# A three-part kernel on one core: work recorded as operations and list-scheduled inside the kernel, in place of loops ordered by the compiler's scheduler

## The chip, the core and the metric

The kernel runs on one core of a Trainium2 chip. The core has five engines that run on their own: TensorE (PE in the profile, with its weight loads as PEld), VectorE (DVE), ScalarE (ACT), GpSimd (POOL) and SyncE (SP), which here issues every transfer (DMA). Each engine works through its own queue in order: an instruction that waits holds up all that stands behind it on that engine. The metric is device time of one execution in microseconds (us), lower is better.

## The reference, cut to what matters

```python
scores = q @ k.T / sqrt(64)                  # 2 batches, 8 heads, 576 rows, 64 wide
kth = the 32nd largest score of each row
attn = softmax over the scores >= kth        # the others count as nothing
x = (attn @ v), heads side by side           # 1152 tokens x 512
h = x @ moe_w_in                             # 512 -> 2048
g = h * tanh(softplus(h))
x = g @ moe_w_out                            # 2048 -> 512
out = ((x @ w_a) * (x @ w_b)) @ w_out        # 512 -> 1536 twice, 1536 -> 512
```

Data and results are float32. The weights of both MLPs come to the device as 64-bit words, and the kernel turns them into float32 itself.

## The kernel before, in words

**Tiles.** The 1152 tokens are nine tiles of 128 rows, t = 0 to 8. For every tile attention goes through four pairs of heads, hp = 0 to 3, so there are 36 steps.

**Attention.** `scores` makes the query parts qh and ql and four score products psc for each step (L170), which ACT copies into the tile s2 (L172). `largest` then finds the 32nd largest score with four rounds on DVE: MAX8 (L186) takes the eight largest, MATCH_REPLACE8 (L189) strikes them out. That makes 8 MAX8 and 6 MATCH_REPLACE8 in each step. `weighted_sum` masks and exponentiates (L206 on DVE, L192, L211 and L212 on ACT), transposes on PE (pe, L219), multiplies by v (px, L225 and L228), and after the fourth pair divides by the sums: prs on PE (L240), then x on DVE (L242). In this document x3 and x8 are the results x of the fourth and of the ninth tile.

**Weights.** `convert` reads each of 68 weight blocks (128 x 512, 512 KB as 64-bit words), turns it into float32 and stores it to device memory (ws, 256 KB): two or three ACT instructions (L285, L286, L289), a shift on DVE (L287), then an integer add and a multiply by the sign on POOL (L290, L291). For nine blocks DVE merges the sign instead (L293). `weight` loads a stored block again (raw, 256 KB) each time that a group of tiles needs it. For the tiles that use split operands it makes two parts of it, whl: a high part by a cast (L321 on ACT or L319 on DVE) and the rest by a subtraction (L322 on POOL or DVE). Which engine does it follows counters (`phase`, `sub`).

**MLPs.** SEQ is the list of groups: the gated MLP (kind 1) for tiles 0, 1 and 2, each alone and unsplit, then the bilinear MLP (kind 2) for tiles 0 to 2 together, gated for 3 to 5, bilinear for 3 to 5, gated for 6 to 8, bilinear for 6 to 8. From the first bilinear group on operands are split, three matmuls for one product. The products are ph (L349), the sums acc and po (L363, L371). The gate's multiplication is L410 in the gated MLP and L445 in the bilinear one; `gate_parts` splits the result into gh (ACT, L378) and gl (L379).

**Order.** Three sources of work (attention, conversion, MLP) are generators. A loop at the end of the kernel keeps a clock of DVE, ACT and PE, with rounded costs (PACE, `cost`), and steps the source whose clock is lowest. The compiler's own scheduler then orders the instructions of all engines by priority (`tc.high_priority(PRI[...])`) and by its own model of time; it also moves single matmuls between each other.

Of the kernel before, what the change touches and what calls it, by code (L numbers as in the profile page):

```python
# [9 lines left out]
F32 = mybir.dt.float32  # L10
# [8 lines left out]
P = 128  # L19
U = 512  # L20
TOPK = 32


SEQ = [(1, [0], 0, 0, 1, 0), (1, [1], 0, 0, 4, 0), (1, [2], 0, 0, 0, 0), (2, [0, 1, 2], 1, 4, 0, 0), (1, [3, 4, 5], 1, 4, 0, 0), (2, [3, 4, 5], 1, 4, 1, 0), (1, [6, 7, 8], 1, 4, 4, 2), (2, [6, 7, 8], 1, 4, 0, 1)]

PACE = (2.8, 1.0, 0.8, 1.65, 0.315, 0.0, 16.0)

PRI = (200, 444, 30, 0, 37, 100)

PS = (3, 2, 3)  # L30


KSUB = (0, 0)

SIGN = (4, 3)

ABUF = (5, 3, 2, 1, 2, 3, 1, 2)
BUFS = (3, 9, 9, 6, 1)

WIDE = {2 * P: 2, P: 4}  # L40
NEG = -3.0e38
STEEP = 2.0 ** 100
# [3 lines left out]
def topk_attention_mlps(ctx: ExitStack, tc: tile.TileContext, q, k, v, w, out):  # L46
# [9 lines left out]
    F1, F2 = 16, 12  # L56
# [8 lines left out]
    const = ctx.enter_context(tc.tile_pool(name="const", bufs=1))  # L65
    stg = ctx.enter_context(tc.tile_pool(name="stg", bufs=2))
    att = ctx.enter_context(tc.tile_pool(name="att", bufs=2))
    xp = ctx.enter_context(tc.tile_pool(name="xp", bufs=1))
    wp = ctx.enter_context(tc.tile_pool(name="wp", bufs=1))
    ep = ctx.enter_context(tc.tile_pool(name="ep", bufs=ABUF[5]))  # L70
    dp = ctx.enter_context(tc.tile_pool(name="dp", bufs=1, space=DRAM))
    ps = ctx.enter_context(tc.tile_pool(name="ps", bufs=PS[0], space=PSUM))
    ps_h = ctx.enter_context(tc.tile_pool(name="ps_h", bufs=PS[1], space=PSUM))
    ps_a = ctx.enter_context(tc.tile_pool(name="ps_a", bufs=PS[2], space=PSUM))

    kks = const.tile([P, H + 2, S], F32R, name="kks")
# [3 lines left out]
    nc.vector.memset(half, 0.5)  # L80

    def bank(name, n=512):
        return ps.tile([P, n], F32, name=name, tag="bank", padded_shape=[P, 512])

    nc.scalar.preload_act_table_set("natural_log_exp_and_others")
    vt, v4, KK, QQ, X, XR = {}, {}, {}, {}, {}, {}

    def load_v(b):
        vt[b] = const.tile([P, H, J, D], F32, name=f"v{b}")
        v4[b] = const.tile([P, NP, 2, D], F32, name=f"v4{b}")  # L90
        nc.gpsimd.memset(v4[b], 0.0)
        for h in range(H):
            nc.sync.dma_start(vt[b][:, h], v[b, h, 0:SM, :].rearrange("(p j) d -> p j d", j=J))
        for s in range(2):
            nc.sync.dma_start(
                v4[b][s * R:(s + 1) * R, :, s, :],
                v[b, :, SM:S, :].rearrange("(a s) p d -> s p a d", s=2)[s],
            )

    def prep_k(b, hp):  # L100
        ks = wp.tile([P, 2, J, D], F32, name="ks", bufs=BUFS[4])
        kr = wp.tile([R, 2, D], F32, name="kr", bufs=BUFS[4])
        for s in range(2):
            nc.sync.dma_start(ks[:, s], k[b, 2 * hp + s, 0:SM, :].rearrange("(p j) d -> p j d", j=J))
        nc.sync.dma_start(kr, k[b, 2 * hp:2 * hp + 2, SM:S, :].rearrange("h p d -> p h d"))
        km = wp.tile([P, 2, J, 2, D], F32R, name="km", bufs=BUFS[4])
        kn = wp.tile([R, 2, 2, D], F32R, name="kn", bufs=BUFS[4])
        for z, raw in ((km, ks), (kn, kr)):
            high, low = (z[..., i, :] for i in range(2))
            nc.scalar.copy(high, raw)  # L110
            (nc.gpsimd, nc.vector)[KSUB[b]].tensor_sub(low, raw, high.bitcast(F32))
        for s in range(2):
            kk = kks[:, (b * H + 2 * hp + s) % (H + 2), :]
            pk = bank("pk")
            for j in range(J):
                nc.tensor.transpose(pk[:, j * P:(j + 1) * P], km[:, s, j].rearrange("p z d -> p (z d)").bitcast(F32),
                                    ident)
            pr = bank("pr", R)
            nc.tensor.transpose(pr, kn[:, s].rearrange("p z d -> p (z d)").bitcast(F32), ident[:R, :R])
            for src, o, n in ((pk, s * R, SM), (pr, SM * (1 - s), R)):  # L120
                nc.scalar.copy(kk[:, o:o + n], src)  # L121
            KK[b, 2 * hp + s] = kk

    def load_q(t):
        qr = stg.tile([P, H, 2, D], F32, name="qr", bufs=1)
        for z in range(2):
            if t == J:
                for b in range(B):
                    nc.sync.dma_start(qr[b * R:(b + 1) * R, :, z, :], q[b, :, SM:S, :].rearrange("h p d -> p h d"))
            else:  # L130
                rows = q[t // (J + 1), :, 0:SM, :].rearrange("h (p j) d -> j p h d", j=J)
                nc.sync.dma_start(qr[:, :, z, :], rows[t % (J + 1)])
        QQ[t] = qr

    def prep_q(t, hp):
        pq = bank("pq", 2 * P).rearrange("p (s t) -> p s t", t=P)
        for s in range(2):
            nc.tensor.transpose(pq[:, s, :], QQ[t][:, 2 * hp + s, :, :].rearrange("p z d -> p (z d)"), ident)
        made = []
        for b, o, n in ([(t // (J + 1), 0, P)] if t != J else [(b, b * R, R) for b in range(B)]):  # L140
            qh = att.tile([P, 2, P], F32R, name="qh", bufs=ABUF[4])
            ql = att.tile([P, 2, P], F32R, name="ql", bufs=ABUF[4])
            if n != P:
                z = slice((1 - b) * R, (2 - b) * R)
                nc.gpsimd.memset(qh[:, :, z].bitcast(F32), 0.0)
                nc.gpsimd.memset(ql[:, :, z].bitcast(F32), 0.0)
            dh, dl, src = (z[:, :, o:o + n] for z in (qh, ql, pq))
            nc.scalar.mul(dh, src, SCALE)
            nc.vector.scalar_tensor_tensor(dl, src, SCALE, dh.bitcast(F32), op0=ALU.mult, op1=ALU.subtract)
            made.append((b, qh, ql))  # L150
        return made

    def scores(t, hp):
        with tc.high_priority(PRI[0]):
            return scores_(t, hp)

    def scores_(t, hp):
        if hp == 0:
            load_q(t)
        made = prep_q(t, hp)  # L160
        if t in (0, J):
            prep_k(t // J, hp)
        s2 = att.tile([P, 2, S], F32, name="s2", bufs=ABUF[0])
        for s in range(2):
            h = 2 * hp + s
            parts = [(qq, KK[b, h]) for b, qh, ql in made for qq in (qh, ql)]
            for a in range(2):
                psc = bank("psc", HS)
                for n, (qq, kk) in enumerate(parts):
                    nc.tensor.matmul(psc, qq[:, s, :], kk[:, a * HS:(a + 1) * HS],  # L170
                                     start=(n == 0), stop=(n == len(parts) - 1))
# [407 lines left out]
```

## Time and profile before

| | before |
|---|---|
| median of three runs | 774.36 us (770.68 to 776.7) |
| the profiled execution's own time | 773.75 us |
| its span, first to last instruction | 771.9 us |
| busy: PE / DVE / ACT / POOL | 679.2 / 581.2 / 542.2 / 469.3 us |
| granted clock of PE, mean | 0.956 |
| moved by DMA | 131.37 MB |

How to read the rows. A group of instructions stands in one line: its line in the kernel, engine, operation, output and inputs by the program's names, count, time busy and mean time of one. What is to the right of an arrow to the left (<-) after an idle time is what ended that idle time. A table by stretches gives for each engine how long it was busy in that stretch and how many instructions it had. Matmuls overlap, so the time of one is longer than the distance to the next.

### The profile page before, as it was taken

How to read it: one execution, taken by the hardware profiler on the slowest of the kernel's cores; microseconds unless marked ns; L12 is line 12 of the kernel's file. 1: busy time of each engine (PE TensorE's matmuls, PEld its weight loads, DVE VectorE, ACT ScalarE, POOL GpSimd, SP SyncE). 2: the span in 40 equal slices, each digit the busy share in tenths (PEclk: the TensorE clock that was granted, in tenths of full speed). 3: DMA queues.
4: the chain of work that ended last, by engine and by line, in shares of the span. 5: the costliest groups of instructions: out<-in, count | busy, mean ns of one | idle time of the engine just before them, and what ended most of it. 6: DMA issues, size and time to landing. Idle time of an engine off the chain costs nothing.

```text
span 771.9 us, 12517 instructions
## 1 busy us (share of the span) xinstructions
PE 679.2 (88%) x4072; PEld 574.7 (74%) x4072; DVE 581.2 (75%) x1148; ACT 542.2 (70%) x1161; POOL 469.3 (61%) x449
## 2 busy tenths in 40 slices
PE   3475777789889978999997899989999999999997
PEld 2354645566667648989987788868888999999996
DVE  2999998998999998776779998995782277642131
ACT  5888797997988788566666898876564356564442
POOL 6776767685656577655652566663665564566561
PEclk9969969888999989999999999999999999999999
DMA  8887799889899888323432332522350354444411
GB/s 243 284 246 236 224 277 320 278 271 312 292 317 324 277 301 257 110 69 103 118 96 71 76 87 83 137 69 69 83 169 37 80 171 125 129 125 123 125 53 42
DMA packets 82417, 131.37 MB, mean 170 GB/s; under 512 B 27824, under 2 KB 31920, under 8 KB 82352
## 3 DMA queue, kind: packets, MB, share of 16 engines
q1 hardware_dynamic: 82352, 130.58, 55.2%
q8 instruction: 32, 0.52, 0.3%
q14 instruction: 33, 0.27, 0.1%
HBM read 110.36 MB, written 20.19 MB: 169 GB/s over the span
## 4 chain that ended last, share of the span: by engine, by line
PE 59%; DVE 18%; DMA 10%; ACT 7%; issue 4%; POOL 2%; SPq 1%; ACTq 0%; POOLq 0%; DVEq 0%
PE ph L349 29%; PE po L363 9%; DVE m L186 7%; DVE wk L189 6%; DMA w<-in_w_dram 5%; PE acc L363 4%; PE px L225 4%; PE acc L371 4%; PE psc L170 3%; DMA raw<-ws 3%; PE pe L219 2%; DVE w L287 2%; DMA ws<-w 2%; PE px L228 1%; DVE e L206 1%
## 5 line engine op out<-in xcount | busy, mean ns | idle before, releaser
L322 POOL TENSOR_TENSOR whl<-raw,whl 128x512 fp32r<-128x512 f32 x150 | 200.7, 1346 | 117.8 <-ACT whl L321 88.9
L186 DVE MAX8 m<-wk 128x8 f32<-128x576 f32 x216 | 158.6, 749 | 0.9
L349 PE MATMUL ph<-yh,whl 128*128 128x384 f32 x576 | 156.3, 340 | 0.1
L290 POOL TENSOR_TENSOR w<-w,w 128x512 int32<-128x512 int32 x59 | 76.7, 1300 | 58.4 <-DVE w L287 24.8
L349 PEld LDWEIGHTS ph<-yh,whl 128*128 128x128 f32 x576 | 104.5, 188 | 3.2 <-ACT yh L423 0.4
L189 DVE MATCH_REPLACE8 wk<-m,wk 128x576 f32<-128x576 f32 x144 | 106.4, 741 | 0.0
L349 PE MATMUL ph<-yl,whl 128*128 128x384 f32 x288 | 97.2, 338 | 0.1
L321 ACT CAST whl<-raw 128x512 fp32r<-128x512 f32 x125 | 76.5, 622 | 27.4 <-PE po L363 13.1
L186 DVE MAX8 m<-s 128x8 f32<-128x576 f32 x72 | 54.0, 751 | 37.4 <-ACT s L172 37.2
L291 POOL TENSOR_TENSOR w<-w,w 128x512 f32<-128x512 f32 x59 | 79.5, 1351 | 3.9 <-ACT xr L230 1.2
L225 PE MATMUL px<-et,v 128*64 128x128 f32 (+1 forms) x640 | 64.3, 290 | 18.6 <-ACT et L220 18.6
L379 POOL TENSOR_TENSOR gl<-m,gh 128x384 fp32r<-128x384 f32 x48 | 52.0, 1083 | 44.2 <-ACT gh L378 16.7
L349 PE MATMUL ph<-xh,whl 128*128 128x384 f32 x256 | 71.8, 342 | 0.9 <-DVE m L410 0.9
L225 PEld LDWEIGHTS px<-et,v 128*64 128x64 f32 x640 | 42.1, 144 | 37.5 <-ACT et L220 24.8
L172 ACT COPY s<-psc 128x288 f32<-128x288 f32 x144 | 52.0, 401 | 21.6 <-PE psc L170 21.1
L170 PE MATMUL psc<-kks,qh 128*128 128x288 f32 x160 | 52.2, 346 | 14.8 <-ACT kks L121 6.7
L220 ACT COPY et<-pe 128x384 f32<-128x384 f32 x108 | 49.1, 484 | 18.4 <-PE pe L219 17.9
L445 DVE TENSOR_TENSOR m<-ph,e 128x384 f32<-128x384 f32 x36 | 19.9, 552 | 53.4 <-PE ph L349 49.6
L285 ACT ACTIVATE w<-w 128x512 f32<-128x512 f32 x68 | 46.3, 681 | 16.3 <-DMA w<-in_w_dram 14.6
L363 PE MATMUL po<-whl,gh 128*128 128x512 f32 x216 | 57.5, 397 | 0.0
L378 ACT CAST gh<-m 128x384 fp32r<-128x384 f32 x68 | 34.8, 512 | 32.1 <-DVE m L445 15.1
L219 PE MATMUL pe<-ident,e 128*128 128x128 f32 x324 | 51.6, 289 | 5.9 <-ACT s L172 5.3
(99 smaller groups left out, 1581.4 us busy)
## 6 DMA issues: line engine op xcount, KB each, us to landing
raw<-ws SPq DMA_DIRECT2D x249, 256.0 KB, 2.9
w<-in_w_dram SPq DMA_DIRECT2D x68, 512.0 KB, 5.2
ws<-w SPq DMA_DIRECT2D x68, 256.0 KB, 5.4
qr<-in_q_dram SPq DMA_DIRECT2D x16, 256.0 KB, 4.1
ks<-in_k_dram SPq DMA_DIRECT2D x16, 128.0 KB, 3.8
v<-in_v_dram SPq DMA_DIRECT2D x16, 128.0 KB, 3.9
out_dram<-o SPq DMA_DIRECT2D x8, 256.0 KB, 2.4
qr<-in_q_dram SPq DMA_DIRECT2D x4, 128.0 KB, 5.5
```

The costliest lines, as they stand in the source:

```text
L170: nc.tensor.matmul(psc, qq[:, s, :], kk[:, a * HS:(a + 1) * HS], start=(n == 0), stop=(n == len(parts) - 1))
L172: nc.scalar.copy(s2[:, s, a * HS:(a + 1) * HS], psc)
L186: nc.vector.max(m8[:, s, got], src[:, s, :])
L189: nc.vector.match_replace(wk[:, s, :], m8[:, s, got], src[:, s, :], NEG)
L219: nc.tensor.transpose(pe[:, i, :], ef[:, n * P:(n + 1) * P], ident)
L225: nc.tensor.matmul(px[s * D:(s + 1) * D, o:o + n], vt[b][:, 2 * hp + s, j, :], et[:, s * (J + 1) + j, o:o + n], start=(j == 0), stop=False ...
L290: nc.gpsimd.tensor_tensor(wi, wi, count, op=ALU.add)
L291: nc.gpsimd.tensor_mul(wf, wf, highf)
L321: nc.scalar.copy(wh, raw)
L322: sub().tensor_sub(wl, raw, wh.bitcast(F32))
L349: nc.tensor.matmul(ph, a, x, start=(i == 0), stop=(i == len(mm) - 1))
L363: nc.tensor.matmul(acc[i], z[:, i * P:(i + 1) * P], a, start=(first and m == 0), stop=(last and m == len(mm) - 1))
```

## The change

The kernel computes the same thing with the same SEQ, the same number and sizes of PE instructions and nearly the same instructions elsewhere. What is new is how the order is made. Every operation is recorded first (`Plan.add`) with the engines it may run on, a cost in nanoseconds for each, a priority, and the buffers it reads and writes. `Plan.run` then goes through time by events. For each free engine it takes, among the operations whose inputs are done and whose buffers are free, the one with the lowest priority number. It models DMA as a wire of 330 bytes a nanosecond with 2.2 us behind it, a lag after each operation, and a lock between DVE and POOL for operations marked so. An operation that two engines may do goes to the one that is free first. `Plan.emit` writes the instructions out in that order inside `tc.manual_schedule()`, so the compiler's scheduler keeps it. The priorities are places on a time line: ATT by tile for attention, CONV for conversion, MLP for each group, with an offset by kind of work (BIAS).

The constants of the order (CAPS) keep the buffer counts of before, but for gh and gl, two in place of one.

Work that moves between engines, by the counts of the two built programs: subtractions of whl on DVE 16 before and 97 now (POOL 156 and 75), casts of whl on DVE 41 and 68 (ACT 131 and 104), the shift of the conversion on DVE 68 and 17, the other 51 as an integer multiply by eight on POOL. The nine sign merges on DVE are gone, with three more sign passes on ACT for each four (204 against 195 ACT instructions of the conversion) and nine more multiplies on POOL. Reloads of stored blocks are 260 in place of 249.

```diff
+ATT = (-1.5, 56.7, 86.6, 129.7, 174.6, 267.2, 298.9, 351.6, 396.9, 428.2)
+CONV = (-3.6, 25.1, 119.5, 209.4, 336.8)
+MLP = ((122.6, 134.3), (77.1, 211.3), (174.5, 210.4), (231.0, 353.2), (353.8, 387.1), (441.9, 588.2), (602.3,
+        686.5), (611.0, 705.0))
...
+            for e in LAG:
+                while free[e] <= now + 1e-9 and ready[e]:
+                    best = None
+                    for o in ready[e]:
+                        p = o.prio
+                        cost, locks = o.engines[e]
+                        if locks:
+                            other = lock["POOL" if e == "DVE" else "DVE"]
+                            if other > now:
+                                p += LOCKED * (other - now) / 1e3
+                        if len(o.engines) > 1:
+                            p += SHIFT[e]
+                        if best is not None and (p, o.index) >= (best[0], best[1].index):
+                            continue
...
+                    if e == "SP":
+                        free[e] = now + 60.0
+                        wire = max(wire, now) + cost / 330.0
+                        o.end = wire + LAG[e]
...
+    def minus(prio, dst, a, b, n, reads, writes):
+        add({"POOL": (70.0 + 2.31 * n, True), "DVE": (70.0 + 1.04 * n, True)}, prio,
+            lambda e: ENG[e].tensor_sub(dst(), a(), b()), reads, writes)
...
+        def shift(e, wi=wi):
+            if e == "DVE":
+                nc.vector.tensor_scalar(wi(), wi(), 3, 0x7FFFFFFF, op0=ALU.logical_shift_left, op1=ALU.bitwise_and)
             else:
+                nc.gpsimd.tensor_tensor(wi(), wi(), eight.to_broadcast([P, U]), op=ALU.mult)
+
+        add({"DVE": (330.0, True), "POOL": (1250.0, True)}, pr, shift, [(wf, 0)], [(wf, 0)])
...
-                nc.vector.scalar_tensor_tensor(wi, high, -0x80000000, wi, op0=ALU.bitwise_and, op1=ALU.bitwise_or)
...
+    started = plan.run()
+    with tc.manual_schedule():
+        plan.emit(started)
```

What this does to the order is shown at three places. The first is DVE while the fourth tile is searched and weights are converted. In a row, m is the list of the largest scores, wk the scores with the largest struck out, s the scores. Before:

```order
L287 TENSOR_SCALAR w<-w 128x512
L149 SCALAR_TENSOR_TENSOR ql<-pq,qh 128x2x64
L189 MATCH_REPLACE wk<-m_2637,wk 128x576
L206 SCALAR_TENSOR_TENSOR e_2406,sm<-s_2158,m_2408,e_2406 128x576
L405 TENSOR_SCALAR e_2712<-ph 128x512
L189 MATCH_REPLACE wk<-m_2637,wk 128x576
L186 MAX m_2637<-wk 128x8
L287 TENSOR_SCALAR w<-w 128x512
```

Now, at the same part of the search:

```order
L394 MATCH_REPLACE wk<-m_2383,wk 128x576
L418 SCALAR_TENSOR_TENSOR e_2520,sm<-s_1829,m_2383,e_2520 128x576
L390 MAX m_2383<-wk 128x8
L390 MAX m_2547<-s_1998 128x8
L504 TENSOR_SCALAR w<-w 128x512
L394 MATCH_REPLACE wk<-m_2547,s_1998 128x576
L390 MAX m_2547<-s_1998 128x8
L390 MAX m_2547<-wk 128x8
L394 MATCH_REPLACE wk<-m_2547,s_1998 128x576
```

The shift (L287 before, L504 now) stood among the searches every few rows; ahead of x3 it stands 62 times before and 14 times now. The second place is POOL in the conversion of the first tile, before:

```order
L191 TENSOR_SCALAR nm<-m_204 128x2
L290 TENSOR_TENSOR w<-w,w_306 128x512
L291 TENSOR_TENSOR w<-w,w_306 128x512
L290 TENSOR_TENSOR w<-w,w_317 128x512
L291 TENSOR_TENSOR w<-w,w_317 128x512
```

and now, where L506 is the multiply by eight:

```order
L506 TENSOR_TENSOR w<-w,eight 128x512
L519 TENSOR_TENSOR w<-w,w_223 128x512
L422 TENSOR_TENSOR dm<-m_207,nm 128x1
L523 TENSOR_TENSOR w<-w,w_223 128x512
L506 TENSOR_TENSOR w<-w,eight 128x512 x2
```

POOL has a third pass of the same tile shape for most blocks. The third place is ACT where the scores of the fourth pair of heads of the fifth tile are copied, s_3258 before and s_2980 now. The copies (L172, now L258) fill the buffer s that DVE searches; the activation L192, now L415, follows the first round of the search on the buffer that it names. Before:

```order
L172 COPY s_3258<-psc 128x288 x3
L321 CAST whl<-raw 128x512
L444 COPY e_3330<-ph 128x384
L321 CAST whl<-raw 128x512
L172 COPY s_3258<-psc 128x288
L220 COPY et<-pe 128x384 x2
L321 CAST whl<-raw 128x512 x2
L220 COPY et<-pe 128x384
L192 ACTIVATE e_3493<-s_3258,nm 128x576
```

Now:

```order
L258 COPY s_2980<-psc 128x288
L638 ACTIVATE m_3017<-e_2957 128x512
L258 COPY s_2980<-psc 128x288
L415 ACTIVATE e_3025<-s_2404,nm 128x576
L258 COPY xr<-px 128x128
L496 ACTIVATE w<-w_2864 128x512
L258 COPY s_2980<-psc 128x288
```

Before, the copies of s_3258 are the last to be made before s_3258 itself is used. Now they lie around the activation on s_2404, the second pair of the same tile: the scores are made two steps ahead of their search.

Between the last prs (L240, now L472) and the end, PE has 748 matmuls of 384 columns and 152 of 512 before, 816 and 171 now, with six transposes more. Ahead of x3 SP issues 63 loads of 512 KB, 60 stores and 88 reloads of 256 KB before, all with the loads of q, k and v 79.2 MB; now 52, 49 and 86, all together 70.0 MB.

## Rows read from the trace of the kernel before

**Rows 1.** Stretches: us, then PE, PEld, DVE, ACT, POOL busy, clock, DMA share, GB/s

```profile
0.00:278.50 278.50, 209.17 (x1239) 154.53 (x1239) 254.58 (x514) 233.77 (x501) 183.68 (x190) 0.90 0.89 281
278.50:603.30 324.80, 306.37 (x1948) 264.78 (x1949) 254.04 (x515) 225.52 (x500) 192.24 (x190) 0.98 0.36 106
603.30:772.00 168.70, 163.64 (x887) 155.40 (x885) 72.61 (x123) 82.94 (x161) 93.39 (x70) 1.00 0.39 111
200.00:250.00 50.00, 44.35 (x310) 34.25 (x308) 50.00 (x102) 44.81 (x98) 29.07 (x36) 1.00 0.96 312
```

**Rows 2.** The instructions of line L242 (ns min/median/max, first and last start), and x3

```profile
L242 DVE TENSOR_TENSOR x<-xr,prs x9: 661/677/689, 82.7 to 602.6; 128x512 f32<-128x512 f32 x9
...
277.87 0.67 DVE L242 TENSOR_TENSOR x<-xr,prs 128x512 f32<-128x512 f32 x1
```

**Rows 3.** Timeline: the last prs and the last matmuls (start, us)

```profile
598.55 0.27 PE L240 MATMUL prs<-ident,rs 128*64 128x128 f32 x1
...
766.42 0.86 PE L363 MATMUL po<-whl,gl 128*128 128x512 f32 x3
```

**Rows 4.** Waits of DVE from 278.5 to 603.3: us, times, longest

```profile
DVE m L186 <- ACT s L172: 29.9, 14, 5.1
DVE x L242 <- ACT xr L230: 13.0, 3, 9.9
DVE m L445 <- PE ph L349: 6.1, 4, 2.8
DVE rs L235 <- ACT e L212: 5.4, 2, 3.4
```

**Rows 5.** Timeline of DVE where a search waits for its scores

```profile
324.63 0.76 DVE L186 MAX8 m<-wk 128x8 f32<-128x576 f32 x1
328.29 0.76 DVE L186 MAX8 m<-s 128x8 f32<-128x576 f32 x1 [2.90 <-ACT s L172]
```

**Rows 6.** Chain that ended last: start, us, matmuls issued without a gap

```profile
632.23 2.08 PE ph L349 x12
637.77 2.08 PE acc L371 x12
700.26 2.08 PE po L363 x9
```

**Rows 7.** Single lines: ns min/median/max, first and last start

```profile
L322 DVE TENSOR_TENSOR whl<-raw,whl x16: 682/693/1666, 615.9 to 676.9; 128x512 fp32r<-128x512 f32 x16
L319 DVE CAST whl<-raw x41: 408/420/1527, 512.3 to 679.9; 128x512 fp32r<-128x512 f32 x41
L379 DVE TENSOR_TENSOR gl<-m,gh x20: 551/559/1558, 639.6 to 765.1; 128x384 fp32r<-128x384 f32 x20
L287 DVE TENSOR_SCALAR w<-w x68: 377/426/1918, 8.2 to 303.7; 128x512 int32<-128x512 int32 x68
L290 POOL TENSOR_TENSOR w<-w,w x59: 1284/1296/1474, 8.8 to 303.1; 128x512 int32<-128x512 int32 x59
L322 POOL TENSOR_TENSOR whl<-raw,whl x150: 1270/1294/1822, 301.8 to 755.7; 128x512 fp32r<-128x512 f32 x150
```

**Rows 8.** Stretch to x3, line L287 alone: us, DVE busy (instructions)

```profile
0.00:278.50 278.50, 40.54 (x61) 0.90 0.89 281
```

**Rows 9.** Groups by shape: count, busy us, mean ns, idle time before

```profile
L186 DVE MAX8 m<-wk 128x8 f32<-128x576 f32 x216 | 158.6, 749 | 0.9
L189 DVE MATCH_REPLACE8 wk<-m,wk 128x576 f32<-128x576 f32 x144 | 106.4, 741 | 0.0
L322 DVE TENSOR_TENSOR whl<-raw,whl 128x512 fp32r<-128x512 f32 x16 | 16.2, 1010 | 0.3
L293 DVE SCALAR_TENSOR_TENSOR w<-w,w 128x512 int32<-128x512 int32 x9 | 8.9, 990 | 0.1
L285 ACT ACTIVATE w<-w 128x512 f32<-128x512 f32 x68 | 46.3, 681 | 16.3 <-DMA w<-in_w_dram 14.6
```

**Rows 10.** DMA issues: count, KB each, median us to landing

```profile
raw<-ws SPq DMA_DIRECT2D x249, 256.0 KB, 2.9
w<-in_w_dram SPq DMA_DIRECT2D x68, 512.0 KB, 5.2
```

More of the change, by code (lines that the diff above doesn't have):

```diff
@@ L153, in scores @@
[L153 to L166, printed above, removed]
-            for a in range(2):
[L168 to L171, printed above, removed]
-                nc.scalar.copy(s2[:, s, a * HS:(a + 1) * HS], psc)
-        return s2
@@ L300, in weight @@
-    def weight(*a):
-        with tc.high_priority(PRI[3]):
-            return weight_(*a)
-    def weight_(split, *key):
-        made[3] = max(made[3], order.index(key))
-        convert(order.index(key) + 1)
+                    nc.tensor.matmul(prs()[o:o + D, h // 2 * P:(h // 2 + 1) * P],
+                                     rs()[:, h:h + 1].to_broadcast([P, D]), ident, start=True, stop=True,
+                                     skip_group_check=True)
+            add(one("PE", 850.0), pr, spread, [(rs, 0)], [(prs, 0)], [x])
@@ new lines, in weighted_sum @@
+            add(one("DVE", 600.0), pr,
+                lambda e: nc.vector.tensor_mul(x(), xr(), prs().rearrange("p (c t) -> p c t", t=P)),
+                [(xr, None), (prs, 0)], [(x, 0)])
+    steps = [(t, hp) for t in range(S * B // P) for hp in range(NP)]
+    for t, hp in steps:
+        at = ATT[t] + (ATT[t + 1] - ATT[t]) * hp / NP
+        s2 = scores(t, hp, at)
+        weighted_sum(t, hp, at, s2, *largest(s2, at))
+    order = [(z, f, i) for z, F in ((0, F1), (1, F2)) for f in range(F) for i in range(2 + z)]
@@ L352, in finishing, with product, mult @@
+    def product(pr, wz, xz, T, ph, o):
+        def mult(e):
+            mm = [(value(a)[:, c * P:(c + 1) * P], x(c)) for c in range(NC) for a, x in pairs(wz, [z[1] for z in xz])]
+            for i, (a, x) in enumerate(mm):
+                nc.tensor.matmul(ph()[:, o:o + T], a, x, start=(i == 0), stop=(i == len(mm) - 1))
+        rate = NC * (3 * 0.4525 * T if len(wz) == 2 else 2 * 0.84 * T)
+        add(one("PE", rate), pr, mult, reads(wz) + [z[0] for z in xz], [(ph, o)])
     def finishing(n, parts, last):
@@ L460, in results @@
-    def results(tiles, split):
-        return parts(xp, [P, NC, len(tiles) * P], "y", split, bufs=2)
-    att_stream = attention()
-    made_at, done_at, home = {}, {}, {}
-    clock = {"DVE": 0.0, "ACT": 0.0, "PE": 0.0}
-    last = max(i for i, z in enumerate(SEQ) if z[0] == 1)
-    def begin(i):
-        kind, tiles, split, second, copies, subs = SEQ[i]
-        phase[:] = copies, subs
-        made[2] = i
-        if kind == 2:
-            return bilinear(tiles, home[tiles[0]][0], split, second)
-        if tiles[0] not in home:
-            group = next(z for z in SEQ if z[0] == 2 and tiles[0] in z[1])
-            yt = results(group[1], group[2])
-            home.update({t: (yt, j) for j, t in enumerate(group[1])})
-        return gated(tiles, *home[tiles[0]], split, second, i == last)
@@ L480, in cost @@
-    def cost(i):
-        kind, tiles, split, *_ = SEQ[i]
-        n = len(tiles)
-        unit = 0.16 * n
-        if kind == 1:
-            pe = unit * (7.5 if not split else 8 if i == last else 8)
-            return pe, 0.31 * n, (0.6 + 0.14 * split) * n + split
-        return 12 * unit, 0.16 * n, 0.28 * n + 1.5
-    def attend():
-        before = set(X)
-        clock["PE"] = max(clock["PE"], clock["DVE"] - PACE[6]) + PACE[2]
-        clock["DVE"] += PACE[0]
-        clock["ACT"] = max(clock["ACT"], clock["DVE"] - 2 * PACE[6]) + PACE[1]
-        more = next(att_stream, False) is None
-        for t in set(X) - before:
-            made_at[t] = clock["DVE"]
-        return more
```

813 lines of the change are left out of this document (491 added, 322 removed).

## The prediction

> **What bounds the kernel now.** I read the end of the trace first, since there one engine is alone. The last prs ends at 598.8 and the last matmul at 767.3 [rows 3], and between them PE issues without a gap: twelve matmuls of 384 columns or nine of 512 in 2.08 us [rows 6], that is 0.173 and 0.231 us each. The 748 and 152 matmuls of that stretch make 129.6 + 35.1 = 165 us of the 168.5. So behind the last tile of attention PE is the bound, and the reader sees what it has left there.
>
> Then I read the stretches [rows 1]. Up to x3, which ends at 278.5 [rows 2], DVE is busy for 254.6 us. It is the engine that sets the pace, but ACT (233.8) and the transfers (0.89 of the time, 281 GB/s) are close behind, so shortening DVE alone would not give all that it saves. PE's clock is 0.90 there, and PE has room.
>
> From x3 to x8 PE is busy for 306 of 325 us and DVE for 254. The two do not wait for the same thing: PE has products to do, while DVE stands idle for 70.8 us. The waits of DVE say why [rows 4]: 29.9 us are spent by the search waiting for scores that ACT copies just before [rows 5]. They come late because their matmuls stand behind MLP products in PE's queue. Each such wait puts off x8, and with it the end, since x8 opens the last gated group. So the span is four parts: 278.5 to x3, 320.3 to the last prs, 168.5 to the last matmul, 4.6 to the end, together 771.9 us. The profiled execution took 773.75, and the median of the runs is 774.36, that is 2.5 above the span.
>
> **To x3.** The change takes 48 of 62 shifts from DVE. In the trace 61 of them take 40.5 us, 0.665 each [rows 8]: −31.9. Six sign merges at 0.99 [rows 9]: −5.9. The search is less far ahead at x3 by seven MAX8 and five MATCH_REPLACE8 [rows 9]: −8.9. Five subtractions of k come to DVE at 0.69 (the same two-input form, [rows 7]), +3.5, and smaller edits take about as much away. DVE: 254.6 − 46.7 = 208. With the 24 us of idle time that it has there now, x3 would be done at 232.
>
> POOL takes 36 of the multiplies by eight in this stretch. No row shows an integer multiply there. The nearest is the integer add of the same shape, 1.28 to 1.47, median 1.30 [rows 7]; I take 1.30, since it is the same engine, shape and type, and keep twice that for a rival. It loses fifteen passes of the conversion, six of whl and four of k at about 1.3: 183.7 + 46.8 − 32.5 = 198. ACT has eleven blocks less to convert, about three passes of 0.68 each [rows 9]: 233.8 − 22 = 212. Both are hidden behind DVE, if with little to spare.
>
> SP issues 70.0 MB ahead of x3 in place of 79.2, since eleven blocks are converted later, each 512 KB in, 256 KB out [rows 10]. At the 281 GB/s of this stretch that takes 249 us, at the 312 of its densest part [rows 1] 224. So x3 lies between 232, if DVE goes on setting the pace, and 249, if the transfers do. I take the middle, 241. The eleven blocks are not saved: they come where the transfers take 0.36 of the time, so there they are hidden.
>
> The page GPSIMD Engine Reference (Engine selection) of the Trainium skill says that two-input work on tiles belongs on VectorE, since GpSimd is about twice as slow at it. The trace agrees, and more: 0.43 against 1.30 us at the median [rows 7], so by that rule the 51 moved shifts cost 44 us of engine time. It does not change the sum, because POOL is idle for 95 us of this stretch and DVE is not.
>
> **From x3 to the last prs.** DVE gets work here: 19 subtractions of whl at 1.01 (the mean, [rows 9]; 0.69 when nothing holds them up), +19.2; twelve casts at 0.42 and fourteen gl at 0.56 [rows 7], +12.8; the search that was not done ahead, +8.9; it loses four shifts and three merges, −6. That is 254 + 35 = 289. Its waits: of 70.8 us the 29.9 for scores go, because the copies now stand two steps ahead of their use, and a step has 14 searches of about 0.74 us [rows 9]. What is late next is the end of each tile, where x waits for xr and rs for the sums [rows 4]; 9.9 of that lie behind the last prs and outside this part. 31 us of waits remain if none of them shrinks, which makes 320; none makes 289. I take the middle, 304.
>
> PE gives a second account of the same part. It sends 16.8 us of its work to the last part (below) and takes 5.4 from the first; with its present stalls it would need 320.3 − 11.4 = 309. The two agree well enough.
>
> **The last part.** PE has 68 more matmuls of 384 columns, 19 of 512 and six transposes there: 11.8 + 4.4 + 0.6 = +16.8, so 185.3. What feeds it shifts from POOL to DVE: 62 more subtractions at 0.69 to 1.01 and 15 more casts, less 17 gl, put DVE at 72.6 + 40 to 60, at most 133 of 185 us. That is hidden behind PE as long as no product has to wait for its whl.
>
> **Sum.** 241 + 304 + 185.3 + 4.6 = 735, and 2.5 between span and median: **737 us**, against 774.36.
>
> **Rivals.** *The order fits better than I give it credit for.* DVE keeps the pace to x3 (232) and waits for nothing after it (289): 232 + 289 + 185.3 + 7.1 = 713. For it: scores are ahead, and PE, DVE and ACT have near-equal work in the middle part. Against it: all queues are in order, and the plan's wire of 330 GB/s is faster than any stretch here [rows 1].
>
> *POOL becomes the bound of the first stretch.* If the multiply takes two passes, 2.6 us, POOL has 198 + 47 = 245 us there, and with the idle time that DVE has now x3 comes at 269: 269 + 304 + 192.4 = 765, at the edge of no change. Nothing in the profile speaks for two passes; that it is a new form speaks against certainty.
>
> *The waits come back elsewhere.* Transfers set x3 (249), the middle part keeps 320, and in the last part ten products wait a microsecond each for a whl that DVE has not made: 249 + 320 + 195 + 7 = 771, no change. For it: whole products are now one unit in PE's order, where single matmuls used to be moved into gaps. Against: the 29.9 us.
>
> *DVE and POOL hold each other up, and it is slower.* In the middle part the forms of [rows 7] that show long maxima on DVE (subtractions, casts, gl, shifts, merges, and the masking L206) grow from 35 to 77. If each of the 42 more waited out a whole POOL instruction of 1.30 us, that is 55 us on DVE: 304 + 55 = 359, and the time is 792. It passes 774 once the wait is 0.9 us each. So far it is a third of that: mean 1.01 against median 0.69 for the subtraction, 0.665 against 0.43 for the shift [rows 7 to 9].
>
> The Trainium skill (SBUF — State Buffer, Who interferes with whom) states this as a rule: a VectorE instruction with two SBUF inputs, or in a two-port mode, and a GpSimd one that reads SBUF exclude each other for a whole instruction. The trace agrees in the maxima, a subtraction of 0.69 that takes 1.67 us [rows 7].
>
> **How the numbers follow.** The forecast, 737 with its own spread of 720 to 760, has a chance of 0.55; the better fit 0.20; POOL 0.10; the waits that come back 0.08; the lock 0.07. A measurement of this kernel can tell about 1% from no change, so 766.6 and 782 are the edges. Faster: 0.55 + 0.20 + half of POOL = 0.80. No change: the other half and the waits, 0.13. Slower: 0.07. The range goes from the better fit, 713, to the upper edge of what forecast and POOL give, 768; it leaves out the slower case, most of the waits that come back, and times below the better fit.
>
> **What would show it.** Right: x3 at 232 to 249 with DVE busy for some 208 us until then; L504 on DVE in a few rows only; the waits of the search for scores near zero after x3; the last prs near 545; 185 us from there to the last matmul without a gap. Wrong: the multiply L506 well over 1.3 us; subtractions on DVE at a mean near 2 us; PE waiting for whl in the last part; ACT or SP standing still in the first stretch behind a load that has not landed, which my sum has only in the bound of 249.

## The result and the profile after

The changed kernel takes 711.13 us at the median (706.8 to 716.44) against 774.35 for the kernel before: a ratio of 0.919, interval 0.912 to 0.926. It is faster, as forecast, but by 63 us instead of 37; the time lies 2 us under the low end of the range. The profiled execution took 711.34 us with a span of 709.1.

The stretches of the kernel after, cut at its own x3 and last prs (columns as in [rows 1]):

```profile
0.00:237.00 237.00, 183.75 (x1228) 144.28 (x1229) 215.02 (x445) 212.88 (x471) 188.45 (x198) 0.91 0.92 293
237.00:519.60 282.60, 275.03 (x1836) 242.93 (x1835) 279.07 (x563) 232.33 (x517) 203.45 (x193) 0.99 0.50 155
519.60:709.10 189.50, 184.18 (x1012) 175.39 (x1011) 112.72 (x189) 82.66 (x161) 37.04 (x33) 1.00 0.39 111
```

The four parts of the sum (the middle part is x3 to the last prs, the last part goes on to the last matmul):

| part, us | before | forecast | after |
|---|---|---|---|
| to x3 | 278.5 | 241 | 237.0 |
| middle | 320.3 | 304 | 282.6 |
| last part | 168.5 | 185.3 | 185.7 |
| tail | 4.6 | 4.6 | 3.8 |
| span | 771.9 | 735 | 709.1 |

The middle row of the stretches holds the surprise. DVE is busy for 279.1 of 282.6 us, where it was busy for 254 of 325 [rows 1]. The waits of DVE there, in the form of [rows 4], are all but gone:

```profile
DVE m L688 <- PE ph L558: 2.0, 3, 0.9
DVE ql L351 <- ACT qh L348: 0.6, 1, 0.6
...
DVE x L478 <- ACT xr L258: 0.2, 1, 0.2
```

L688, L390 and L478 are now what L445, L186 and L242 were; L235 has gone to ACT. The 29.9 us of the search for scores have no row left: by the timelines of ACT and DVE the last copy of a step's scores ends 32 us ahead of that step's search, at the median of this part, where before it ended 3.6 us after the search had begun on the first of its two heads. But the others shrank as well: the 13.0 of x to 0.2, the 6.1 of the products to 2.0, the 5.4 of rs to nothing. Ahead of x3 the search still waits for 5.6 us:

```profile
DVE m L390 <- ACT s L258: 5.6, 2, 3.5
```

Groups by shape (as in [rows 9]): the integer add on POOL, the subtraction of whl on DVE, the multiply by eight on POOL, the cast of whl on DVE.

```profile
L519 POOL TENSOR_TENSOR w<-w,w 128x512 int32<-128x512 int32 x68 | 92.6, 1363 | 21.2 <-issue 7.6 <-ACT w L499 5.5 <-DVE w L504 3.4
L263 DVE TENSOR_TENSOR whl<-raw,whl 128x512 fp32r<-128x512 f32 x97 | 72.5, 747 | 4.5 <-ACT whl L258 1.8
L506 POOL TENSOR_TENSOR w<-w,eight 128x512 int32<-128x512 int32 x51 | 58.0, 1137 | 17.2 <-ACT w L496 15.2 <-DMA raw<-ws 1.9
L258 DVE CAST whl<-raw 128x512 fp32r<-128x512 f32 x68 | 33.5, 493 | 30.8 <-PE ph L558 12.3 <-PE po L581 10.0 <-PE acc L579 8.5
```

The multiply took 1.14 us on average, less than the 1.30 taken for it. The 97 subtractions took 0.75 over the whole span, where the sixteen of before took 1.01 [rows 9].

That DVE's busy time rose by less than its work shows in its timeline, in a stretch of the search without a gap:

```profile
399.89 0.74 DVE L390 MAX8 m<-s 128x8 f32<-128x576 f32 x1
400.56 0.79 DVE L418 SCALAR_TENSOR_TENSOR e<-s,m,e 128x576 f32<-128x576 f32 x1
401.28 0.08 DVE L418 DVE_READ_ACCUMULATOR e<-s,m,e 128x1 f32 x1
401.28 0.41 DVE L258 CAST whl<-raw 128x512 fp32r<-128x512 f32 x1
401.62 0.75 DVE L390 MAX8 m<-wk 128x8 f32<-128x576 f32 x1
402.29 0.53 DVE L641 SCALAR_TENSOR_TENSOR m<-m,ph 128x384 f32<-128x384 f32 x1
```

The columns are start, duration, engine and line. The MAX8 of 0.74 us starts at 399.89, and the masking behind it at 400.56, so 0.07 us before the MAX8 ends. Each instruction here starts 0.06 to 0.08 us before the one ahead has ended. An instruction in a full queue thus costs its pitch (0.67 for MAX8, 0.34 for the cast), not its duration. The prediction summed durations.

The last part goes as forecast. The chain that ended last (start, us, matmuls without a gap) reads there as [rows 6] did, and of what PE waited for in this stretch there is one row, of 1.5 us:

```profile
690.74 4.18 PE ph L558 x24
694.92 2.08 PE po L581 x9
697.01 4.18 PE ph L558 x24
701.19 4.14 PE po L581 x18
```

```profile
PE ph L558 <- DVE yl L655: 1.5, 1, 1.5
```

### The profile page after: what moved, and what is told of

It reads as the page before. It is cut to its first block, busy times and chain, and to the rows that moved or that the text cites. A ratio compares the mean times of both kernels' runs of the same rounds, so it can differ in the third digit from the quotient of the medians.

```text
span 709.1 us, 12496 instructions
## 1 busy us (share of the span) xinstructions
PE 643.0 (91%) x4072; PEld 562.6 (79%) x4072; DVE 606.8 (86%) x1194; ACT 527.9 (74%) x1149; POOL 428.9 (60%) x423
## 4 chain that ended last, share of the span: by engine, by line
PE 49%; DVE 20%; ACT 14%; DMA 9%; issue 4%; POOL 4%; SPq 0%; POOLq 0%; DVEq 0%; ACTq 0%
PE ph L558 24%; PE po L581 9%; DVE m L390 7%; DVE wk L394 6%; PE acc L579 5%; DMA w<-in_w_dram 3%; DMA raw<-ws 3%; PE acc L581 3%; PE psc L372 2%; ACT e L638 2%; DMA ws<-w 2%; PE px L450 2%; ACT w L496 2%; PE pe L438 2%; ACT w L499 1%
## 5 line engine op out<-in xcount | busy, mean ns | idle before, releaser
L390 DVE MAX8 m<-wk 128x8 f32<-128x576 f32 x216 | 154.8, 743 | 0.0
L263 POOL TENSOR_TENSOR whl<-raw,whl 128x512 fp32r<-128x512 f32 x75 | 100.3, 1344 | 50.7 <-ACT whl L258 22.6
L519 POOL TENSOR_TENSOR w<-w,w 128x512 int32<-128x512 int32 x68 | 92.6, 1363 | 21.2 <-issue 7.6
L258 ACT CAST whl<-raw 128x512 fp32r<-128x512 f32 x104 | 63.8, 623 | 34.2 <-PE ph L558 30.2
L263 DVE TENSOR_TENSOR whl<-raw,whl 128x512 fp32r<-128x512 f32 x97 | 72.5, 747 | 4.5 <-ACT whl L258 1.8
L506 POOL TENSOR_TENSOR w<-w,eight 128x512 int32<-128x512 int32 x51 | 58.0, 1137 | 17.2 <-ACT w L496 15.2
L438 PEld LDWEIGHTS pe<-ident,e 128*128 128x128 f32 x324 | 40.7, 147 | 26.1 <-issue 9.5
L258 DVE CAST whl<-raw 128x512 fp32r<-128x512 f32 x68 | 33.5, 493 | 30.8 <-PE ph L558 12.3
L258 ACT COPY e<-ph 128x384 f32<-128x384 f32 x36 | 17.3, 481 | 56.1 <-PE ph L558 56.1
L638 ACT ACTIVATE e<-e 128x384 f32<-128x384 f32 (+1 forms) x88 | 48.9, 555 | 13.5 <-DVE e L633 12.7
L558 PEld LDWEIGHTS ph<-yl,whl 128*128 128x128 f32 x288 | 55.1, 191 | 4.2 <-DVE yl L655 1.9
L258 ACT COPY s<-psc 128x288 f32<-128x288 f32 x144 | 52.7, 406 | 7.3 <-PE psc L372 6.9
L372 PE MATMUL psc<-kk,qh 128*128 128x288 f32 x160 | 56.1, 364 | 1.0 <-DVE ql L351 0.8
```

The source lines that it names most:

```text
L258: add(eng, prio, lambda e: nc.scalar.copy(dst(), src()) if e == "ACT" else nc.vector.tensor_copy(dst(), src()), reads, writes)
L263: lambda e: ENG[e].tensor_sub(dst(), a(), b()), reads, writes)
L372: nc.tensor.matmul(psc()[:, :HS], qq()[:, s, :], kk()[:, a * HS:(a + 1) * HS], start=(n == 0), stop=(n == len(heads) - 1))
L390: lambda e, s=s, src=src, got=got: nc.vector.max(m8()[:, s, got], src()[:, s, :]),
L438: nc.tensor.transpose(pe()[:, i * P:(i + 1) * P], ef[:, n * P:(n + 1) * P], ident)
L506: nc.gpsimd.tensor_tensor(wi(), wi(), eight.to_broadcast([P, U]), op=ALU.mult)
```

## The experiments

The prediction's theory, called A: the scores are made two steps ahead of their search, so the waits for them go, and with them some 30 us; the shift on POOL gives the first part. Rival B: no single edit gives the gain. It comes from one order over all queues that is kept as planned, made with costs that match the chip. The numbers of the priorities (ATT, CONV, MLP, BIAS) stay in every test of the changed kernel as they are, but for e6 and e11; with numbers made for each test a loss could be smaller. A table of all parts stands at the end of the section.

**e1: the look-ahead alone cut down.** Two buffers for scores in place of five, planned again.

```diff
-..."whl": 6, "s2": 5, "wk": 3,...
+..."whl": 6, "s2": 2, "wk": 3,...
```

> The changed kernel with two score buffers in place of five (s2 in CAPS), the plan made anew: scores can no longer be made two steps ahead of the search. Theory A (the gain between x3 and the last prs, 320 to 283 us, is the search no longer waiting for its scores): the waits of the search for score copies come back, 20 to 30 us, that part takes 305 to 315, and the time is 733 to 745. Rival B (the gain is the work moved between engines and the order as a whole): the part stays under 290 and the time under 718.

727.66 us (ratio 0.942, 0.939 to 0.944): 16.5 us of the 63 are lost, a time between those of A and B. But they are not lost where A looks for them. Waits of DVE in the middle part:

```profile
DVE ql L351 <- ACT qh L348: 2.5, 5, 1.4
DVE m L688 <- PE ph L558: 2.2, 6, 0.8
DVE gl L263 <- ACT gh L258: 1.1, 1, 1.1
DVE m L390 <- ACT s L258: 0.6, 1, 0.6
```

The look-ahead is down to one step at most: the last copy of a step ends 3.7 us ahead of its search at the median, in after 32. The search waits 0.6 us, not 29.9, and the middle part takes 279.4 us. What is lost lies ahead of x3 (+10.2), where DVE has 10.6 us more to do (225.6 against 215.0), and in the last part (+8.6), for which more of PE's work is left. So the waits for scores go without a look-ahead of two steps; that scores have to come ahead of their search at all is not refuted by this run.

**e3: the look-ahead alone added.** The kernel before, whose loop writes the scores out four steps ahead in place of two; the five buffers stay.

```diff
-ABUF = (5, 3, 2, 1, 2, 3, 1, 2)
+ABUF = (5, 3, 2, 1, 2, 3, 1, 4)
```

> The kernel before with one number changed: attention makes the scores of four steps ahead in place of two (the last number of ABUF). Theory A: the search's waits for scores between x3 and x8, 29.9 us before, fall below 10, and the time to 745 to 757. If scores that come earlier only push PE's products back, or the waits go to other tiles, the time stays within 1% of 774.

811.58 us, 5% slower than before (1.051, 1.049 to 1.054) and outside both forecasts. Waits of DVE, first up to x3, then in the middle part:

```profile
DVE w L287 <- ACT w L285: 23.6, 12, 5.3
...
DVE m L186 <- ACT s L172: 2.0, 1, 2.0
```

```profile
DVE e L206 <- ACT e L192: 34.1, 12, 8.7
DVE m L445 <- PE ph L349: 15.6, 6, 8.3
DVE yl L333 <- ACT yh L331: 7.4, 3, 6.2
```

The waits for scores do go, as A says (the last copy of a step now ends 7 us ahead of its search), and the time does not: what DVE waits for next is also made by ACT, the conversion's first pass and the exponentials. The middle part is 24 us shorter than before, but DVE has 29 us less to do in it and still stands idle for 73 us there. Ahead of x3 DVE has 20.5 us more to do, and all 68 blocks are loaded there, 63 before. So the removed waits came back under other names, with some 38 us more; how much of that is the earlier conversion was not taken apart.

**e10: keep an order, but without a plan.** The loop of before, in the order it is written, with the compiler's scheduler off.

```diff
+    ctx.enter_context(tc.manual_schedule())
     attending, i, f, stream = True, 0, 0, None
```

> The kernel before in the order in which its loop writes the work out, kept as it is (a manual schedule, no plan): the scores stand 14 to 28 us of VectorE work ahead of the search, but all 68 blocks are loaded ahead of x3. Theory C (it is the compiler's reordering that costs, any kept order gains): below 765. Theory D (it is the plan's knowledge of when inputs and buffers are ready that gains; a coarse order without it leaves engines waiting): 790 or more.

1758.88 us, 2.27 times before. Waits of DVE over the whole span:

```profile
DVE w L287 <- ACT w L285: 313.2, 48, 11.1
DVE e L405 <- PE ph L349: 253.1, 43, 13.4
DVE m L445 <- PE ph L349: 251.0, 36, 12.4
```

The scores stand 46 us ahead of their search here, but these three lines stand right behind what they need, and DVE waits. PE's granted clock is 0.72 at the mean, 0.956 before, and PE is busy for 888 us in place of 679, so the clock may have its part in the loss. Keeping an order does not gain of itself.

**e4: the planned order, not kept.** The recorded operations are emitted in the planned order, and the compiler's scheduler may move them again.

```diff
-    with tc.manual_schedule():
-        plan.emit(started)
+    plan.emit(started)
```

> The changed kernel emitted in the same order, but not inside the manual schedule: the compiler's scheduler is free to reorder it again, with the choice of engines as planned. Theory C (keeping the planned order is what gains): the score copies slide back towards their use and the time is 740 or more. Rival B (engines and numbers of work are what gains): 711 to 722.

800.81 us (1.036, 1.033 to 1.040): 90 us more than after, and slower than before, with the same instructions on the same engines. This is C's side (740 or more), by far. The middle stretch, and what DVE waits for in it:

```profile
283.70:609.80 326.10, 293.84 (x1838) 249.25 (x1836) 263.29 (x534) 216.06 (x479) 152.98 (x157) 0.96 0.36 110
```

```profile
DVE whl L263 <- ACT whl L258: 14.6, 3, 6.4
DVE e L418 <- ACT e L415: 11.4, 6, 2.6
DVE yl L602 <- ACT yh L258: 11.1, 4, 6.5
DVE m L688 <- PE ph L558: 9.2, 7, 3.5
```

DVE stands idle for 62.8 of 326.1 us, nearly the 66.9 of before up to its last prs, now for other things; for scores it is 4.1 us. 63 blocks are loaded ahead of x3, as before the change, where the plan has 52. So the engine moves do not gain without their order. How much of the 90 us is the earlier conversion and how much the rest was not taken apart; e6 prices 60 blocks ahead of x3 under a plan.

**e6: the conversion planned early.** Later places of CONV drawn forward.

```diff
-CONV = (-3.6, 25.1, 119.5, 209.4, 336.8)
+CONV = (-3.6, 25.1, 100.0, 150.0, 190.0)
```

> The changed kernel with the conversion's time line pulled in (the last three numbers of CONV), the plan made anew: 60 blocks instead of 52 are loaded ahead of x3, 76 MB instead of 70. If putting off the conversion is what shortens the first stretch, x3 comes at 255 to 262 instead of 237 and the time at 722 to 735, since the eight blocks' work is gone from where there was room. If the plan absorbs it, the time stays below 717.

731.52 us (0.947, 0.941 to 0.952), 20 us more than after. x3 comes 22 us later, with DVE busy for 232.0 us until then. The middle part is 15 us shorter and the last 13 longer: work that DVE and PE do early or late changes place, and x3's delay stays. So eight of the eleven blocks that after converts later are priced at 22 us of x3, a little more than the shift in e2 below. The two prices were taken one by one and need not add up to the 41.5 us by which x3 came earlier.

**e2: the shift on DVE again.**

```diff
-        add({"DVE": (330.0, True), "POOL": (1250.0, True)}, pr, shift, [(wf, 0)], [(wf, 0)])
+        add(one("DVE", 330.0, True), pr, shift, [(wf, 0)], [(wf, 0)])
```

> The changed kernel with the conversion's shift on VectorE alone, all 68, the plan made anew. If VectorE's work sets x3 (237 now), 35 more shifts at 0.43 to 0.67 us ahead of it bring x3 to 252 to 260, and the time to 726 to 734. If the transfers set x3, it stays below 245 and the time below 719.

730.95 us (0.948, 0.944 to 0.952). Its first stretch:

```profile
0.00:256.20 256.20, 201.45 (x1262) 154.41 (x1263) 228.18 (x483) 217.59 (x480) 152.60 (x163) 0.90 0.87 276
```

DVE has 13 us more to do, POOL 36 less, and x3 comes 19 us later; the DMA share falls from 0.92 to 0.87. So ahead of x3 DVE sets the pace and the transfers follow it. The Trainium skill (GPSIMD Engine Reference, Engine selection) advises VectorE for an elementwise multiply on a tile and puts GpSimd at about twice the time for two inputs. The trace agrees with the factor where the work is the same: the subtraction of whl takes 0.69 us at the median on DVE and 1.29 on POOL [rows 7]. Here the choice of VectorE still costs 20 us, since it is the engine that the others wait for.

**e5: that move alone, in the kernel before.** Fifty shifts as a multiply on POOL.

```diff
+            if len(stored) % 4 and len(stored) < 67:
+                nc.gpsimd.tensor_tensor(wi, wi, eight.to_broadcast([P, U]), op=ALU.mult)
+            else:
```

> The kernel before with 50 of the 68 shifts as a multiply by eight on POOL, its order still made by the compiler's scheduler: one part of the change alone. If VectorE's work sets x3 in the kernel before too (254.6 of 278.5 us busy), 42 shifts less at 0.665 bring x3 to some 252 and the time to 744 to 752. If the scheduler gives it back (it loads 67 blocks ahead of x3 here, 81 MB, 288 us at 281 GB/s), x3 stays above 270 and the time within 1% of 773.

794.95 us, slower (1.029, 1.023 to 1.034) and outside both forecasts. Up to x3 DVE is busy for 245.9 us in place of 254.6, and x3 comes at 297.8. The largest wait of DVE until then, which is 7.3 us in the kernel before:

```profile
DVE m L188 <- ACT s L174: 29.1, 11, 6.5
```

The 44 shifts fewer ahead of x3 are 28 us by their durations, but DVE is busy for only 9 less: the masking takes 1.34 us at the mean there, 0.99 before, the sign merges 1.13, 0.78 before. And it waits 22 us more for scores. The compiler's scheduler also loads all 68 blocks ahead of x3 here, 63 before. The same move that is worth 20 us in the plan costs 22 outside it.

**e7: the plan without the lock.** The model no longer holds DVE and POOL apart.

```diff
-                        lock[e] = at + cost
+                        pass
...
-LOCKED = 81.4
+LOCKED = 0.0
```

> The changed kernel whose plan knows nothing of the lock between VectorE and GpSimd (the lock's time is not kept and its penalty is zero). If planning around the lock matters, the mean of a whl subtraction on VectorE goes from 0.75 to 0.9 us or more, waits open up, and the time is 720 to 735. If not, 706 to 716.

745.12 us (0.965, 0.959 to 0.970), 34 more than after and worse than I expected of either theory. The middle stretch, and the two groups on DVE that grew most:

```profile
240.30:544.40 304.10, 277.47 (x1806) 240.94 (x1806) 299.04 (x584) 219.60 (x488) 186.66 (x177) 0.97 0.46 142
```

```profile
L263 DVE TENSOR_TENSOR whl<-raw,whl 128x512 fp32r<-128x512 f32 x106 | 84.3, 795 | 6.0 <-ACT whl L258 3.1 <-POOL dm L422 0.7
L258 DVE CAST whl<-raw 128x512 fp32r<-128x512 f32 x92 | 49.1, 534 | 32.6 <-PE ph L558 15.7 <-PE po L581 12.4 <-PE acc L579 4.5
```

Here the middle part takes the 304 us that I had forecast, but as work: DVE is busy for 299. The single instruction is only a little slower (0.795 against 0.747 for the subtraction, 0.534 against 0.493 for the cast). More of it is choice: a plan that thinks DVE's casts and subtractions undisturbed gives DVE more of them (92 casts and 106 subtractions, after: 68 and 97), and of the 24 casts more, 20 stand in the middle part.

**e12: the plan with wrong costs.** The search's two instructions priced a quarter too low; nothing else.

```diff
-                add(one("DVE", 660.0), pr,
+                add(one("DVE", 495.0), pr,
...
-                    add(one("DVE", 728.0), pr,
+                    add(one("DVE", 546.0), pr,
```

> The changed kernel whose plan believes that the search costs three quarters of what it does (495 and 546 ns in place of 660 and 728). If a plan needs costs that are right, VectorE gets work that it has no time for (37 subtractions and 41 casts between x3 and the last prs, in place of 19 and 19), waits open up and the time is 730 to 760. If the order alone matters, 708 to 722.

770.23 us (0.995, 0.993 to 0.998): half a per cent under before, so nearly the whole gain is lost, more than I expected even of B. Its first two stretches:

```profile
0.00:256.10 256.10, 185.48 (x1167) 143.50 (x1167) 231.40 (x479) 209.89 (x464) 172.36 (x186) 0.87 0.82 257
256.10:561.00 304.90, 276.21 (x1799) 239.34 (x1799) 291.36 (x578) 219.78 (x490) 173.96 (x165) 0.98 0.49 154
```

DVE is busy for 16 and 12 us more in them, and POOL for 16 and 29 less: a plan that takes DVE for faster than it is loads the engine that is already the bound, in the middle part with 14 subtractions and 20 casts of whl more. This is the sharpest test between the theories: buffers, operations and the keeping of the planned order are as in after, 51 blocks are loaded ahead of x3 (52 in after), and one pair of numbers takes the gain away.

**e11: costs corrected by the trace.** The costs of the subtraction, cast, search, masking and the POOL passes set to what the trace of after shows, the wire to 315, and small steps in the priorities. Two of these edits:

```diff
-            eng["DVE"] = (330.0, True)
+            eng["DVE"] = (400.0, True)
...
-        add({"POOL": (70.0 + 2.31 * n, True), "DVE": (70.0 + 1.04 * n, True)}, prio,
+        add({"POOL": (70.0 + 2.31 * n, True), "DVE": (80.0 + 1.18 * n, True)}, prio,
```

> The changed kernel with the plan's costs set to what the traces show (MAX8 682, MATCH_REPLACE8 738, subtraction on VectorE 0.68 us, the multiply by eight 1.06, transfers 315 GB/s) and small steps of some priorities that the plan then finds better. If the rest of the loss is the plan's error in costs, 697 to 707; if the order is at its limit, 707 to 715.

711.29 us (0.921, 0.918 to 0.924): no difference from after. The costs in the kernel are near enough to the chip; 660 for a MAX8 is its pitch of 0.67 above.

**e9: the subtraction on POOL only.**

```diff
-        minus(pr, lambda: whl()[:, 1, :], raw, lambda: whl()[:, 0, :].bitcast(F32), U, [(raw, 0), (whl, 0)], [(whl, 1)])
+        add(one("POOL", 70.0 + 2.31 * U, True), pr,
```

> The changed kernel with the subtraction of whl on POOL alone (156 there, none on VectorE), the plan made anew: 19 leave VectorE between x3 and the last prs, 78 behind it. If giving them to whichever engine is free matters, POOL has 82 of them, 110 us, in the last part, PE waits for whl there and 9 us more of its work is left for that part: 720 to 735. If it does not matter, 706 to 716.

711.63 us (0.922, 0.917 to 0.926), no difference. The middle part is 11 us shorter and the last 13 longer: DVE has 13 us less to do in the middle, so the last prs comes earlier, and PE takes with it into the last part what it has not yet done. So the 81 subtractions that moved to DVE have no part in the gain that could be measured.

**e8: the limit.** TOPK 24 in place of 32: the fourth round of the search is left out, and the threshold is the 24th largest score.

```diff
-TOPK = 32
+TOPK = 24
```

> The changed kernel with three rounds of search instead of four (the threshold is then the 24th largest score): 72 MAX8 and 72 MATCH_REPLACE8 less, some 105 us of VectorE work, 47 of it ahead of x3; the plan, made anew, moves 24 more subtractions to VectorE. If VectorE sets both stretches, x3 comes near 212, the part behind it near 268, and the time is 685 to 697. If the other engines and the transfers are as close as their sums say (ACT 213, 70 MB at 293 GB/s 239 us), x3 stays above 225 and the time at 700 or more.

707.09 us (0.914, 0.906 to 0.922): 4 us less than after, which the intervals hardly tell apart, for 72 MAX8 and 72 MATCH_REPLACE8 less, 107 us of DVE by their durations. The plan gives DVE other work in their place, so its busy time falls by 52. Its stretches:

```profile
0.00:230.00 230.00, 179.34 (x1202) 140.16 (x1202) 187.87 (x371) 209.09 (x467) 174.06 (x185) 0.88 0.91 291
230.00:496.60 266.60, 260.21 (x1757) 228.63 (x1757) 245.37 (x460) 219.87 (x492) 178.77 (x168) 1.00 0.54 171
496.60:703.50 206.90, 201.55 (x1116) 191.07 (x1116) 121.21 (x204) 88.35 (x173) 39.40 (x35) 1.00 0.37 105
```

Up to x3 ACT and the transfers now stand where DVE stood (209 of 230 us, share 0.91). The middle part gets 16 us shorter, and the last part 17 longer. So DVE is the bound ahead of x3 by a small margin only. Behind x3 it is PE that holds the time, if the middle and the last part are taken together: by the stretches above PE is busy there for 459 us in after, of 468 from x3 to its last matmul, and here for 462 of 470. Before it was 470 of 489. This fits what e6, e9 and this run show, that what DVE is spared in the middle part comes back in the last.

| us | median | to x3 | middle | last part | DVE busy to x3, middle |
|---|---|---|---|---|---|
| before | 774.35 | 278.5 | 320.3 | 168.5 | 254.6, 253.4 |
| after | 711.13 | 237.0 | 282.6 | 185.7 | 215.0, 279.1 |
| e1 two buffers | 727.66 | 247.2 | 279.4 | 194.3 | 225.6, 271.8 |
| e2 shift on DVE | 730.95 | 256.2 | 280.6 | 193.7 | 228.2, 271.3 |
| e6 conversion early | 731.52 | 258.8 | 267.3 | 198.5 | 232.0, 261.1 |
| e7 no lock | 745.12 | 240.3 | 304.1 | 194.3 | 223.7, 299.0 |
| e12 costs off | 770.23 | 256.1 | 304.9 | 200.8 | 231.4, 291.4 |
| e4 order not kept | 800.81 | 283.7 | 326.1 | 185.1 | 236.9, 263.3 |
| e9 subtraction on POOL | 711.63 | 237.5 | 271.5 | 198.8 | 214.0, 266.1 |
| e11 costs corrected | 711.29 | 235.3 | 282.1 | 185.0 | 213.8, 276.8 |
| e8 three rounds | 707.09 | 230.0 | 266.6 | 203.1 | 187.9, 245.4 |
| e3 before, four steps ahead | 811.58 | 323.7 | 296.7 | 183.3 | 275.1, 224.0 |
| e5 before, shift on POOL | 794.95 | 297.8 | 320.6 | 168.4 | 245.9, 243.0 |
| e10 before, program order | 1758.88 | 829.7 | 624.3 | 299.2 | 231.9, 254.0 |

## Why the prediction was right or wrong, point by point

**To x3: right.** 237.0 lies between the 232 and 249 that were given; that it came near their middle, the 241, is luck, for the middle of two bounds is no mechanism. DVE was busy for 215 us (208 forecast) with 22 us idle (24 taken). The durations on DVE fall by 44.8 us, near the 46.7 forecast, but its busy time only by 39.6: there are 69 instructions fewer, and 5.1 us of overlap go with them. ACT was busy for 212.9 (212), POOL for 188.5 (198; the multiply was cheaper, which is 6 of the 9.5). The prediction's 0.43 against 1.30 us for the two engines set a one-input shift beside a two-input add; it did not enter the sum. The transfers ran at 293 GB/s and 0.92 of the time. Which of the two set the pace was left open; e2 settles it for DVE, and e8 shows that ACT and the transfers are only some 7 us behind.

**The middle part: wrong, and this is the step that failed.** I took 304 us, 289 of work and half of 31 us of waits. Measured are 279.1 of work and 3.5 of waits, 21.4 less. Two terms were mis-sized.

The waits are 11.5 us of it. I kept half of the waits for xr, rs and the products of before "if none of them shrinks", and had the search's waits alone go, by the two steps of look-ahead. e1 shows that this was not what it hung on: with a look-ahead of a few us the waits are gone too, and in e3 and e4 the search hardly waits for scores while DVE still stands idle for 73 and 63 us. What sets all these waits at once is the planned order and that it is kept, since e4, with the same instructions in another order, has 62.8 us of idle time on DVE again. Taking waits one by one, as they stood in the trace of before, was the wrong way to count for a change that makes the whole order anew. The 31 us were misread besides. The row of the wait for xr in the trace of before is

```profile
602.62 0.69 DVE L242 TENSOR_TENSOR x<-xr,prs 128x512 f32<-128x512 f32 x1 [9.92 <-ACT xr L230]
```

so the wait began at 592.7, and only 3.8 of its 9.9 us lie behind the last prs at 598.8. Without the scores 37 us were left, and counted so the forecast of this part would have been 307.

The work is the other 9.9 us. The sum of durations that I added, +35, was nearly right: over the instructions that start in the middle part (before up to 603.3, as in [rows 1]) it goes from 280.2 to 312.9 us, +32.7. But the busy time goes from 253.9 to 278.8, only +24.9. The rest, 7.8 us, is overlap: 34.1 us after against 26.3 before, at some 63 ns for each pair that stands back to back (545 pairs, 417 before). Inside the sum the subtractions were cheaper than taken (18 for 15.5 us, 19 for 19.2 forecast) and the masking dearer (1.13 us each, 0.88 before).

PE's second account, 309 us, agreed with the 304 by accident. It kept PE's stalls and its busy time but for the work that moves: the stalls went from 18.4 us (301.9 busy of 320.3) to 7.6, and the busy time fell by 26.8 us where 11.4 were forecast. Over the span it fell from 679 to 643 us for the same matmuls. The clock has a part in it: by the trace's records PE is busy at the lower level of the granted clock (0.5, that is 1.2 GHz) for 58 us before and 37 after. How much of the 36 us that makes, and what the rest is, stays open.

**The last part: right,** 185.7 against 185.3. PE issues without a gap, and whl from DVE (112.7 us busy, at most 133 forecast) holds nothing up.

**Rivals.** The better fit (713, chance 0.20) is what came: x3 at 237 where it had 232, 282.6 where it had 289. That the two errors nearly cancel is luck. The argument against it, that all queues are in order and the plan's wire too fast, was too weak: a wire of 315, with the other changes of e11, leaves the time where it was. POOL as the bound did not come (1.14 us a multiply). Nor did the lock that makes it slower: in the middle part a subtraction takes 0.86 us at the mean, and the masking, dearer by 0.25 us each, comes to 5 us more. But e7 gives the rule that stood beside it (the Trainium skill, SBUF — State Buffer, Who interferes with whom) a price: a plan that ignores it takes 34 us longer. The waits that come back are real in e3, e4 and e5, and absent after.

**The range.** Its low end was a case in which waits are zero and my sum of the work is exact. No room was left for an error of that sum, and it was 10 us too high in the middle part.

**The list of signs.** x3 at 237, no waits for scores after x3 and 185 us without a gap came as listed; the last prs came at 519.6 and not near 545.

## What to carry to other kernels

When a change makes the order of all queues anew, do not carry the waits of the old trace over; work out each engine's own time by part, in pitches from back-to-back rows and not in durations, and let the range reach below the largest of them. A single edit of such a kernel (scores made earlier, a pass moved to an idle engine) can lose more than it gains when the rest of the order does not follow: e3 and e5 lost some 38 and 22 us. An order is as good as the costs behind it: two costs of the engine that sets the pace, a quarter too low, took nearly the whole gain; wrong costs of other engines were not tried. And where a part ends at one engine's work, look at what another still has to do behind it: what DVE was spared in the middle part came back as PE's work in the last.

## What the runs showed of the hardware

Back to back on DVE, an instruction starts 0.06 to 0.08 us before the one ahead ends: MAX8 on 128x576 lasts 0.74 us and costs 0.67.

An integer multiply by a column that is broadcast took 1.14 us on POOL at the mean (128x512), less than the integer add of two whole tiles in the same trace, 1.36; I had kept twice 1.30 as possible.
